# A decode block with a KV cache on one core: eight early stores to the output and two extra loads of x on ScalarE's queue

## The chip, the cores and the metric

The kernel runs on one core of a Trainium2 chip. The metric is the device time of one execution, in microseconds, as the median of several runs. The profile is of one execution of its own, taken by the hardware profiler.

## What is computed

One token per batch row goes through a block: a layer norm of x, attention over a cache of 32768 tokens (32 query heads on 8 heads of keys and values), a gated MLP on the same normed x, and the product of both added to x.

```python
B, Sq, D = 2, 1, 512
Hq, Hkv, Sk, Dh = 32, 8, 32768, 128          # k_cache, v_cache: (B, Hkv, Sk, Dh), float32
...
F = 1792                                     # W_gate, W_up: (D, F); W_down: (F, D)
...
xn = _layernorm(x, axis=-1)
q = (xn @ wq) per head
scores = q k^T * Dh ** -0.5
o = softmax(scores) v
s = o @ wo
gate, up = xn @ W_gate, xn @ W_up
g = silu((gate * (gate > 0) * up) @ W_down)
out = x + s * g
```

The output has 2 x 512 floats, 4 KB.

## The kernel before, in words

The program is written as a list of operations (`pg.op`), each with the engine that carries it out and the names of what it reads and writes. From these names the program works out the semaphore waits: an operation that reads a name waits for the operation that last wrote it, and one that writes a name waits for its last writer and for all who read it since. Each engine then carries out its own operations in the order in which they were listed. A DMA counts on a semaphore of its own (`load(dst, src, sem, ...)` at L239 and L240), 16 for each transfer, and the engine named in `engine=` issues it; all DMA instructions carry the line L240 of the helper, all plain matmuls the line L243.

SyncE (SP) issues all the large loads, in this order: wq (8.4 MB, into `wide`), the first pair of key tiles (8.4 MB, into `k0`), W_gate and W_up (3.7 MB each, into `wide` when the query's products are done with wq), the second pair of key tiles (`k1`), W_down (`load_d`, into `wide` when the gate and up products are done), the third pair of keys, and from there on a pair of value tiles and a pair of key tiles in turn, 32 pairs of each. There are two buffers for keys (`kbuf`) and one for all the rest (`wide`), so a load is issued when its buffer comes free, and waits in the queue behind the loads ahead of it. At the end come the parts of wo and the store of the result.

ScalarE issues the two small loads of x at the start (`xp`, two rows for the layer norm, and `xy`, the same 4 KB in eight rows for the last addition), then takes the square root of the layer norm (L374), later the silu (L648) and the exponentials of the softmax (L722).

The start of the work, as the engines carry it out: VectorE fills constants (`perm`, L291 and L333; `spread` in st3, L341), takes the mean and variance of x (L364 to L372), and behind the square root normalizes x (L378, L380). TensorE turns it (L391) and multiplies by wq in two halves (`project_q`, into m_ps0 and m_ps1). VectorE copies the halves to SBUF (L481: the first into os0, the second into os1), TensorE gathers the heads, VectorE copies them (L498 qd, L517 qall), and GpSimd makes the first group's query qcur (L530). Then VectorE turns the keys in place, 8 transposes for a pair of tiles (L660), TensorE makes the scores, and behind the first two tiles' scores the gate and up products (`mlp_gu`, into m_ps), whose end sets free `wide` for W_down. L580 and the lines behind it make the hidden layer, `mlp_down` and `mlp_fold` the gate g.

os1 is also `ot`, in which each group's heads are turned (L803). perm and st3 are read by TensorE; st3 is written again by the scores of the fourth tile (L678).

Of the kernel before, what the change touches and what calls it, by code (L numbers as in the profile page):

```python
# [8 lines left out]
P = 128  # L9
# [153 lines left out]
def decode_block_kernel(nc, x, kc, vc, wq, wo, wg, wu, wd, out):  # L163
# [17 lines left out]
    def sbuf(name, *shape, align=32):  # L181
        return nc.alloc_sbuf_tensor(name, list(shape), F32, align_bytes=align)[:]
# [6 lines left out]
    st = [sbuf(f"st{i}", P, NR * Q) for i in range(NU)]  # L189
# [7 lines left out]
    perm = sbuf("perm", P, 4, Q // REP, REP)  # L197
# [5 lines left out]
    gy = sbuf("gy", P, P)  # L203
# [18 lines left out]
    ot = os_[1]  # L222
# [7 lines left out]
    def dve(fn, r=(), w=()):  # L230
        pg.op("DVE", fn, r, w)
# [7 lines left out]
    def load(dst, src, sem, r=(), w=(), engine="SP"):  # L239
        pg.op(engine, lambda e: e.dma_start(dst, src), r, w, dma=sem)  # L240
# [22 lines left out]
    def of_columns(t):  # L263
        return t[0:P:APART, :]

    def by_column(t):
        return t.rearrange("b s (c n) -> c (b s) n", c=4)
# [5 lines left out]
            out=ident,  # L273
# [23 lines left out]
    for kb in range(4):  # L297
        dve(
            lambda e, kb=kb: e.memset(block_of[Q * kb : Q * kb + Q, kb * REP : (kb + 1) * REP], 1.0),
            w=["block_of"],  # L300
# [27 lines left out]
    n = 1  # L328
    while n < Q:
# [45 lines left out]
        ["stat", "eps"],  # L375
        ["stat"],
    )
    dve(lambda e: e.reciprocal(stat[:, 4:5], stat[:, 3:4]), ["stat"], ["stat"])  # L378
    dve(
        lambda e: e.tensor_scalar(xc, xc, stat[:, 4:5], None, op0=ALU.mult),  # L380
# [467 lines left out]
    def project_far():  # L848
        parts = []
        for j in range(ROWS - 4, ROWS):  # L850
            parts.append((ots[:, 1, j, :], WO[1][:, j, :], [*its_heads(1), WOK[1, j]]))
        parts.insert(2, (fold, py_sb, ["fold", "os0"]))
        for n, (o, w, held) in enumerate(parts):
            pe(
                chain(
                    [
                        mm(
                            far[32 * c : 32 * c + 32, :P],
                            o,
                            w[:, c * P : (c + 1) * P],  # L860
                            n == 0,
                            n == len(parts) - 1,
                        )
                        for c in range(4)
                    ]
                ),
                held,
                ["s1"],
            )
        dve(lambda e: e.tensor_mul(gy, far[:, :P], gy), ["s1", "gy"], ["gy"])  # L870
        dve(
            lambda e: e.tensor_add(gy, gy, xy),  # L872
            ["gy", "xy"],
            ["gy"],
        )
# [6 lines left out]
    for j in range(PAIRS + 2):  # L882
        s, v = 2 * j, 2 * (j - 2)
# [51 lines left out]

    project_near(range(2, NEAR))
    project_far()
    load(by_column(out), of_columns(gy), "out", r=["gy"])

    sems = {s: nc.alloc_semaphore(f"sem_{s}") for s in pg.count}  # L940
    with nc.Block(no_gpsimd_drain=True) as block:
# [54 lines left out]
```

## Time and profile before

| | us |
|---|---|
| median of 3 runs | 1311.1 (1309.98 to 1311.5) |
| span of the profiled execution, first to last instruction | 1308.4 |
| TensorE busy (matmul) | 859.0 |
| VectorE busy | 718.1 |
| ScalarE busy | 51.4 |
| GpSimd busy | 10.5 |

The profiled execution's own time is known as its span; the median of the runs is 2.7 us longer, which holds what lies ahead of the first and behind the last instruction. The core moves 564.79 MB, at 432 GB/s in the mean over the span. Queue q1 is that of SyncE, q10 that of ScalarE, q8 and q14 carry instructions. In rows of the timeline the first number is the start in us, the second the time it took, and the brackets hold how long the engine had been idle before and what it waited for; SPq and ACTq rows are DMAs being issued. In rows of the DMA queues the numbers are the packets that started in the window asked for, their MB, and the time that they took as a share of the 16 engines' time in that window (over 100% where a packet ends behind the window).

### The profile page before, as it was taken

What the parts mean: (1) busy time and instruction counts of PE and PEld (TensorE: products, weight loads), DVE (VectorE), ACT (ScalarE), POOL (GpSimd) and SP (SyncE); (2) the same over time, 40 slices, a digit from 0 to 9 for tenths busy, and PEclk for the clock granted to TensorE, in tenths of its full rate; (3) what the DMA queues carried; (4) which work ended last, traced back from release to release, by engine and by line L of the source; (5) the groups of instructions that cost most, each with busy time, mean ns of one, the idle gap of its engine ahead of it and who ended that gap; (6) DMA issues with size and microseconds to landing.
All of it is one profiled execution on the core that took longest, in us unless ns stands there. A gap on an engine that the chain in (4) does not pass through costs nothing.

```text
span 1308.4 us, 11146 instructions
## 1 busy us (share of the span) xinstructions
PE 859.0 (66%) x4720; PEld 211.5 (16%) x4720; DVE 718.1 (55%) x690; ACT 51.4 (4%) x133; POOL 10.5 (1%) x38
## 2 busy tenths in 40 slices
PE   3566675785666587576667667667665757865676
PEld 1111111211111121111111112121111112111121
DVE  3566654565655456664546666455665545656521
ACT  0001000000000000000000000000000000000000
POOL 0000000000000000000000000000000000000000
PEclk9677788878878887878898778798887889788788
DMA  9999999999999999999999999999999999999998
GB/s 417 423 438 435 437 431 441 425 439 429 437 429 439 435 433 441 429 441 427 439 429 437 429 439 435 433 441 429 441 427 439 429 437 429 439 435 433 439 431 357
DMA packets 10693, 564.79 MB, mean 432 GB/s; under 512 B 1195, under 2 KB 1211, under 8 KB 1597
## 3 DMA queue, kind: packets, MB, share of 16 engines
q1 hardware_dynamic: 10668, 564.67, 99.7%
q8 instruction: 6, 0.10, 0.0%
q14 instruction: 3, 0.02, 0.0%
q10 hardware_dynamic: 16, 0.01, 0.0%
HBM read 564.67 MB, written 0.00 MB: 432 GB/s over the span
## 4 chain that ended last, share of the span: by engine, by line
DMA 64%; DVE 17%; PE 15%; issue 4%; SPq 0%
DMA k<-in_A_k_cache_dram 58%; DVE k L660 17%; PE o L243 8%; PE s L243 6%; DMA k<-in_A_wo_dram 3%; DMA w<-in_A_wq_dram 2%; PE m_ps L243 1%; PE m_ps L693 0%; PE d L243 0%; SPq L240 0%; DVE gy L870 0%; DVE gy L872 0%
## 5 line engine op out<-in xcount | busy, mean ns | idle before, releaser
L243 PE MATMUL s<-k,qcur 128*32 128x512 f32 x2048 | 504.5, 710 | 370.5 <-DVE k L660 370.3
L660 DVE STREAM_TRANSPOSE k<-k 128x2048 f32<-128x2048 f32 x256 | 565.2, 2275 | 147.0 <-DMA k<-in_A_k_cache_dram 147.0
L243 PE MATMUL o<-w,wt 128*16 128x512 f32 x1984 | 245.5, 596 | 9.0 <-DMA w<-in_A_v_cache_dram 9.0
L243 PEld LDWEIGHTS s<-k,qcur 128*32 128x32 f32 x2048 | 89.5, 123 | 785.0 <-DVE k L660 639.3
L737 DVE STREAM_TRANSPOSE wt<-pt 128x512 f32<-128x512 f32 x64 | 45.9, 717 | 139.4 <-PE pt L243 134.6
L678 DVE TENSOR_SCALAR_CACHE_REDUCE st<-s 128x512 f32<-128x512 f32 x64 | 43.0, 672 | 120.9 <-PE s L243 120.9
L243 PEld LDWEIGHTS o<-w,wt 128*16 128x16 f32 x1984 | 62.4, 98 | 167.5 <-issue 167.5
L722 ACT ACTIVATE st<-st,nb 128x512 f32<-128x512 f32 x64 | 45.4, 710 | 1111.0 <-DVE nb L719 1111.0
L243 PE MATMUL pt<-st,perm 128*128 128x512 f32 x128 | 72.6, 696 | 1.5 <-ACT st L722 1.5
L763 DVE RECIPROCAL rl<-m_ps 128x1 f32<-128x1 f32 x16 | 2.7, 169 | 111.0 <-PE m_ps L243 111.0
L243 PE MATMUL m_ps<-ob,heads 128*128 128x128 f32 x128 | 21.7, 321 | 29.0 <-DVE ob L777 29.0
L243 PEld LDWEIGHTS pt<-st,perm 128*128 128x128 f32 x128 | 25.3, 219 | 34.4 <-issue 30.1
L803 DVE STREAM_TRANSPOSE os<-m_ps 128x512 f32<-128x512 f32 x16 | 11.5, 717 | 23.2 <-PE m_ps L243 23.2
L243 PEld LDWEIGHTS m_ps<-ob,heads 128*128 128x128 f32 x128 | 18.0, 217 | 31.1 <-DVE ob L777 31.1
L243 PE MATMUL m_ps<-w,wt 128*32 128x512 f32 (+1 forms) x128 | 16.2, 640 | 8.1 <-DMA w<-in_A_wq_dram 8.1
L777 DVE SCALAR_TENSOR_TENSOR ob<-o,share,ob 128x128 f32<-128x128 f32 x48 | 16.9, 351 | 1.7
L530 POOL TENSOR_TENSOR qcur<-qall,block_of 128x128 f32<-128x128 f32 x16 | 6.5, 406 | 1008.3 <-PE s L243 974.0
L243 PE MATMUL m_ps<-negone,mrow 1*128 1x1 f32 x32 | 6.0, 256 | 9.3 <-DVE mrow L708 9.3
L722 ACT ACTIVATION_READ_ACCUMULATOR st<-st,nb 128x1 f32 x64 | 11.9, 186 | 0.0
L481 DVE COPY os<-m_ps 128x512 f32<-128x512 f32 x2 | 1.4, 692 | 16.3 <-PE m_ps L243 16.3
L243 PE MATMUL o<-k,wt 128*16 128x512 f32 x64 | 8.4, 687 | 2.8 <-DMA k<-in_A_v_cache_dram 2.8
L391 PE MATMUL m_ps<-ident,st 32*128 32x32 f32 x4 | 0.7, 307 | 14.0 <-DVE st L380 14.0
(80 smaller groups left out, 102.8 us busy)
## 6 DMA issues: line engine op xcount, KB each, us to landing
k<-in_A_wo_dram SPq DMA_DIRECT2D x1, 4096.0 KB, 37.3
w<-in_B_W_gate_dram SPq DMA_DIRECT2D x1, 3584.0 KB, 19.6
w<-in_B_W_up_dram SPq DMA_DIRECT2D x1, 3584.0 KB, 27.6
w<-in_B_W_down_dram SPq DMA_DIRECT2D x1, 3584.0 KB, 15.6
k<-in_A_wo_dram SPq DMA_DIRECT2D x1, 2048.0 KB, 41.7
k<-in_A_wo_dram SPq DMA_DIRECT2D x1, 1024.0 KB, 43.7
k<-in_A_k_cache_dram SPq DMA_DIRECT2D x32, 48.2
k<-in_A_wo_dram SPq DMA_DIRECT2D x1, 512.0 KB, 44.5
```

The lines of the kernel that those rows point to most:

```text
L243: return lambda e: e.matmul(out_, lhs, rhs, start=start, stop=stop, skip_group_check=True)
L391: lambda e, k=k: e.transpose(px[:, k * 32 : (k + 1) * 32], xquad[:, k, :], ident[:32, :32])
L481: dve(lambda e, q=qs, h=half: e.tensor_copy(q, pq[h]), [f"m{half}"], [f"os{half}"])
L530: lambda e: e.tensor_tensor(qcur.rearrange("p e (k h) -> p e k h", h=REP), qall[:, b, hk].unsqueeze(2).to_broadcast([P, 4, Q // REP, REP]) ...
L660: dve(lambda e: e.transpose(at_, at_), [f"k{t // 2 % 2}"], [key])
L678: lambda e: e.tensor_scalar(st[u], ps_s[t % 2], SCALE, None, op0=ALU.mult, op1=ALU.max, accum_out=mx[:, u : u + 1],),
L722: lambda e, u=u: e.activation(st[u], st[u], AF.Exp, bias=nb, scale=1.0, accum_out=ls[:, u : u + 1]),
L737: dve(lambda e: e.transpose(wt[t % 2], ps_p[t % 2]), [f"pt{t % 2}"], [f"wt{t % 2}"])
L763: dve(lambda e: e.reciprocal(rl, ps_m[1][:, :1]), ["m1"], ["rl"])
L777: lambda e, part=part, c=c: e.scalar_tensor_tensor(ob, part, share[:, c : c + 1], ob, op0=ALU.mult, op1=ALU.add),
L803: lambda e: e.transpose(ot, ps_m[1].rearrange("p (h q j) -> p j h q", h=REP, j=ROWS)),
```

## The change

ScalarE issues ten more DMAs behind its square root, in the list of operations between L377 and L378 of before. Eight are stores to the output, in six different shapes of the two sides: from eight rows of perm that lie 16 partitions apart, from the first eight rows of perm, from four rows of it, and from two rows of st3. The two last are loads of x into os1, once into eight rows next to each other and once into rows 16 apart. All ten count on one semaphore, `early`. Each store names "out" as what it writes, each load "os1". The result's store, which overwrites the whole output at the end, now names "out" too. Nothing else is changed.

```diff
+    zeros = perm.rearrange("p a b c -> p (a b c)")
+
+    def in_rows(t):
+        return t.rearrange("b s (c n) -> (b s c) n", c=4)
+
+    def early(dst, src, r, w):
+        load(dst, src, "early", r=r, w=w, engine="ACT")
+
+    one_batch = out[0, 0].rearrange("(c n) -> c n", c=4)
+    early(by_column(out), of_columns(zeros), ["perm"], ["out"])
+    early(by_column(out), of_columns(zeros), ["perm"], ["out"])
+    early(by_column(out), zeros[0:8, :], ["perm"], ["out"])
+    early(in_rows(out), of_columns(zeros), ["perm"], ["out"])
+    early(in_rows(out), zeros[0:8, :], ["perm"], ["out"])
+    early(one_batch, zeros[0:P:32, :], ["perm"], ["out"])
+    early(one_batch, zeros[0:4, :], ["perm"], ["out"])
+    early(out.rearrange("b s d -> (b s) d"), st[3][0:2, :], ["st3"], ["out"])
+    early(ot[0:8, :P], in_rows(x), [], ["os1"])
+    early(of_columns(ot[:, :P]), in_rows(x), [], ["os1"])
     dve(lambda e: e.reciprocal(stat[:, 4:5], stat[:, 3:4]), ["stat"], ["stat"])
...
-    load(by_column(out), of_columns(gy), "out", r=["gy"])
+    load(by_column(out), of_columns(gy), "out", r=["gy"], w=["out"])
```

Here `by_column` is the output's view as 4 x 2 x 128, `of_columns` every 16th partition of a tile. The second writer of os1 in the program's start is VectorE's copy of the query's second half (L481 of before, L500 after the change).

## The prediction

> **What bounds the kernel now.** I read the page first: the share of the DMA, the queues, and the chain of work that ended last.
>
> ```profile
> span 1308.4 us, 11146 instructions
> ...
> DMA  9999999999999999999999999999999999999998
> ...
> q1 hardware_dynamic: 10668, 564.67, 99.7%
> ...
> q10 hardware_dynamic: 16, 0.01, 0.0%
> ...
> DMA 64%; DVE 17%; PE 15%; issue 4%; SPq 0%
> ```
>
> SyncE's queue q1 keeps the 16 DMA engines busy for 99.7% of the span. So the kernel is one stream of 564.67 MB, and time that this stream stands idle can't be made up later. ScalarE's queue q10 carries only the two small loads of x. A change that adds no bytes worth counting can move the time in one way: by making the stream run dry. I therefore ask when the next load must be issued, and on whom it waits. The timeline of the first 45 us shows the start:
>
> ```profile
> 0.74 0.39 SPq L240 DMA_DIRECT2D w<-in_A_wq_dram  x1
> ...
> 1.42 1.19 ACTq L240 DMA_DIRECT2D st<-in_A_x_dram  x1
> ...
> 2.66 0.60 ACTq L240 DMA_DIRECT2D xy<-in_A_x_dram  x1
> ...
> 10.13 0.68 DVE L364 TENSOR_REDUCE stat<-st 32x1 f32<-32x512 f32 x1 [2.91 <-DMA st<-in_A_x_dram]
> ...
> 12.95 0.29 ACT L374 ACTIVATE stat<-stat,eps_t 32x1 f32<-32x1 f32 x1 [8.38 <-DVE stat L372]
> ...
> 32.04 0.69 DVE L481 COPY os<-m_ps 128x512 f32<-128x512 f32 x1 [2.74 <-PE m_ps L243]
> ...
> 33.90 0.22 DVE L498 COPY qd<-pt 128x64 f32<-128x64 f32 x1 [1.16 <-PE pt L243]
> ...
> 35.32 0.42 DVE L517 COPY qall<-pt 128x256 f32<-128x256 f32 x1 [1.20 <-PE pt L243]
> ...
> 43.31 17.66 DVE L660 STREAM_TRANSPOSE k<-k 128x2048 f32<-128x2048 f32 x8 [7.57 <-DMA k<-in_A_k_cache_dram]
> ```
>
> The second L481 (the copy of m_ps1 into os1, at 32.04) is done in time: VectorE is through with the query at 35.74 and then waits 7.57 us for the first keys. The timeline from 60 to 80 us shows the place where the stream first depends on this work:
>
> ```profile
> 66.08 6.28 PE L243 MATMUL m_ps<-w,wt 128*32 128x448 f32 x58
> ...
> 72.39 0.33 SPq L240 DMA_DIRECT2D w<-in_B_W_down_dram  x1
> 72.76 1.28 SPq L240 DMA_DIRECT2D k<-in_A_k_cache_dram  x1
> ...
> 79.54 17.67 DVE L660 STREAM_TRANSPOSE k<-k 128x2048 f32<-128x2048 f32 x8 [4.36 <-DMA k<-in_A_k_cache_dram]
> ```
>
> W_down may only be issued when TensorE has used up the gate and up weights (72.39). The load in flight then, the second pair of keys, lands at 79.5. That is the slack: 7.1 us, less the time from issue to first packet.
>
> **What the change puts where.** On ScalarE ten DMAs come behind the square root (L374 before and after):
>
> ```order
>  L240 DMA xy<-in_A_x_dram 8x1x128 [waits sem_DVE]
>  L374 ACT_TABLE_LOAD
>  L374 ACTIVATE stat<-stat,eps_t 32x1 [waits sem_DVE]
> ...
> +L240 DMA out_dram<-perm 4x2x128
> +L240 DMA out_dram<-perm 4x2x128 [waits sem_early] x2
> +L240 DMA out_dram<-perm 8x128 [waits sem_early] x2
> +L240 DMA out_dram<-perm 4x128 [waits sem_early] x2
> +L240 DMA out_dram<-st 2x512 [waits sem_early]
> +L240 DMA os<-in_A_x_dram 8x128
> +L240 DMA os<-in_A_x_dram 8x128 [waits sem_early]
> ```
>
> Each store but the first waits until the one before has landed, because all of them write "out"; the first load goes right behind the eighth store, the second waits for both. That is nine waits for a landing in a row, counting the last one, which falls to VectorE (L481 of before is L500 of after):
>
> ```order
> -L481 COPY os<-m_ps 128x512 [waits sem_PE] x2
> -L498 COPY qd<-pt 128x64 [waits sem_PE]
> ...
> +L500 COPY os<-m_ps 128x512 [waits sem_PE]
> +L500 COPY os<-m_ps 128x512 [waits sem_early,sem_PE]
> +L517 COPY qd<-pt 128x64 [waits sem_PE]
> ```
>
> The loads write os1, so the copy into os1 waits for all ten. Behind it on VectorE are qd, qall and every transpose of keys; behind those TensorE's scores and the gate and up products; behind these SyncE's issue of W_down. Nothing else waits: ScalarE's own next work, the silu of L648, needs what W_down is multiplied with, and SyncE's last store carries no wait for the early ones, since what VectorE has told it covers them. The ten transfers' bytes (under 40 KB) are nothing beside 564 MB.
>
> Let E be the time at which the tenth transfer has landed. From L481 to the issue of W_down before lie 72.39 - 32.04 = 40.35 us, of which 7.57 were the wait for keys that would be over: 32.8 us of work. After the change W_down is issued at E + 32.8 and its first packets go about 1.0 us later (SyncE's first load was issued at 0.74; the row of 1.7 to 1.8 us, below, holds the first packets). The stream's slowest engine was free at 79.5, the others some 2 us earlier (the row of 76 to 77 us below: three packets start, where 16 engines start one every 2.4 us, so most have begun their last). The stream stands still from there to E + 33.8: a loss of E - 45.7 for the slowest engine and E - 43.8 for the rest, say **E - 45**. Below E = 45 the change is free; this far the wait of 7.57 us and the queue's stock cover it. Once W_down runs, VectorE is 2 us behind the stream's restart, as it was before (77.6 to 79.54), so the rest goes as before, only later.
>
> **What one landing costs.** The trace has two near rows. Without other traffic: the result's store, the same 4x2x128 shape as the first three.
>
> ```profile
> 1306.60 0.69 SPq L240 DMA_DIRECT2D out_dram<-gy  x1
> ```
>
> The span ends at 1308.4, so 1.8 us. Under the stream: x's first load, issued at 1.42 and used at 10.13, so 8.7 us. Nine times the one is 16 us, nine times the other 78. The packets per queue in windows of the trace tell which holds; first 1.7 to 1.8, then q1 and q10 in five windows of 1 us that start at 7.0, 9.4, 11.8, 14.2 and 16.6, then 46 to 48, 76 to 77, and 1306 to 1308.4 us:
>
> ```profile
> q1 hardware_dynamic: 5, 0.33, 979.2%
> ...
> q1 hardware_dynamic: 16, 1.05, 241.9%
> q10 hardware_dynamic: 4, 0.01, 1.4%
> ...
> q1 hardware_dynamic: 16, 1.05, 241.9%
> q10 hardware_dynamic: 4, 0.00, 0.5%
> ...
> q1 hardware_dynamic: 16, 1.05, 241.9%
> q10 hardware_dynamic: 4, 0.00, 0.5%
> ...
> q1 hardware_dynamic: 16, 1.05, 241.8%
> q10 hardware_dynamic: 2, 0.00, 0.3%
> ...
> q1 hardware_dynamic: 16, 1.05, 241.9%
> q10 hardware_dynamic: 2, 0.00, 0.1%
> ...
> q1 hardware_dynamic: 31, 0.89, 102.9%
> ...
> q1 hardware_dynamic: 3, 0.20, 45.4%
> ...
> q1 hardware_dynamic: 12, 0.00, 0.7%
> ```
>
> Each window holds one packet of q1 per engine: 1.05 MB / 16 = 65.5 KB, 2.42 us long. Between two of them an engine serves one packet of q10, however small. The counts 4, 4, 4, 2, 2 fit 2 engines with 1 data packet and 1 closing packet for the first load of x, then 4 engines with 2 and 1 for the second; the result's store has 12 packets, again 4 times (2 + 1). So a transfer under this stream costs one round of 2.42 us per packet, and it has to get in first: x's first load was issued at 1.42, its first packet went in the window at 7.0, so it missed the round one 2.42 us earlier, near 4.8. I read this as one packet of q1 being taken ahead. In a chain the next store is issued about 1.5 us after the last one's closing packet (its closing packet went in the window at 9.4 and the reader began at 10.13, so some tenths until the waiter goes on; 0.6 to issue, as for the second load of x; then the way to the queue, within the 1.0 of SyncE's first load), so it misses the next turn and gets the one after. A two-packet transfer then costs 3 rounds, a three-packet one 4.
>
> Rounds are 2.42 us while wq and keys stream, 1.06 us for the gate and up weights (102.9% x 16 x 2 us / 31). Per engine an 8.4 MB load (128 rows of 64 KB) has 8 packets of 65.5 KB, a gate or up load (3.67 MB in 128 rows) 8 of 28.7 KB (0.89 MB / 31). Counted from the first packets at 1.7 to 1.8, with 8 rounds a load: wq to 21.9, keys to 41.3, gate and up to 58.3, the second keys to 77.7. Now the chain, from the square root's end at 13.24:
>
> Store 1 (three packets) stands behind the second load of x on engines 0 and 1, whose last packet goes near 17: data 19.4 and 21.9, closing with the end of wq, landed between 22 and 24.4. Stores 2 and 3, the same shape: 4 rounds each, about 9.7 us, so about 32 to 34 and 41.4. Stores 4 to 7 have two packets (one row per engine; this count is an estimate from the shapes) and meet the short rounds: 4 x 1.06 = 4.2 us each (the 1.5 us on the way use up two rounds), so 45.6, 49.9, 54.1, 58.3. Store 8 on long rounds: 3 x 2.42 = 7.3, 65.6. The first load follows on the same queue, two rounds more: 70.4. The second load: 7.3 more, **E = 78**. The loss is 78 - 45 = **33 us**: span 1308.4 + 33 = 1341.4, and with the 2.7 us by which the median of the runs (1311.1) lies above this span, **1344 us**. The bounds of a landing are the rows of 1.8 and 8.7 us.
>
> **The rivals.**
>
> *No packet taken ahead.* If a store gets the first turn after it is issued, every long transfer saves one round: 22 to 24, 31, 38, 42, then 3.2 us each in the short rounds (45, 48, 51, 55), the first load 57 and the second 61. E = 61, loss 16: 1327 us. For it: the first load of x may only have been slow on its way (its issue took 1.19 us, the second's 0.60). Against: the second load, too, missed the round near 5, and SyncE's own first packet came within 1.0 us of its issue.
>
> *Each landing costs what it costs on free engines: not slower.* Nine times 1.8 from 13.3 gives 29.5, before L481 at 32.04: 1311 us, no change. This decides as soon as a landing costs under (45 - 13.3) / 9 = 3.5 us in the mean. For it: the q10 packets themselves last hundredths of a us. Against: the windows above, where each waits 2.42 us for its turn, and the 8.7 us of the first load. The Trainium skill has a rule that gives this outcome: "DMA: Bandwidth & Descriptors", Anatomy of one DMA, puts a DMA at about 2.0 us fixed plus its bytes at 436 GB/s; by that estimate the chain ends near 31 and costs nothing. This trace's 8.7 us beside a full stream disagrees with it.
>
> *More than one packet ahead.* Then every landing costs a round more, and the chain meets the end of the stream at 77.7 with transfers left, which then land in 1.8 us each: with two or three left E = 82 to 84, 1348 to 1350 us. For it: nothing beyond the loose fit of one observation. The same skill page, Queues, rings and completion order, says that an engine goes round its queues by whole packets and gives 9 to 17 descriptors as typical for one; were the eight 65.5 KB records of a load one such packet, a turn would take 19 us and this rival would hold. The windows show a q10 packet after each single 65.5 KB record, so I give it little.
>
> That the change doesn't chain its transfers I exclude: the rows above carry the waits, and the value VectorE waits for in the code is that of all ten.
>
> **The numbers.** Forecast (E = 76 to 80) 0.55; no packet ahead, or only some turns missed (E = 58 to 75) 0.26; more ahead 0.11; as on free engines, no change 0.07; faster 0.01, for which I see no mechanism. A measurement of this kernel can tell about 0.2%, 2.6 us, from no change. Slower 0.92, same 0.07, faster 0.01. The range takes the forecast with its bounds, most of the no-packet-ahead case and the lower end of more ahead: 1325 to 1350 us.
>
> **What would show it.** In the timeline of the changed kernel: the second copy into os1 starts near 78 and names a DMA as what it waited for; W_down is issued near 111; a hole in the DMA share of the slices near 80 to 112 us; the stores' issues on ScalarE 4 us apart between 41 and 58 and 7 to 10 us apart elsewhere; after 112 the same pace as before. Issues 2 us apart, or a second copy at 32, would prove me wrong, and so would a hole without the full loss in the time: then the stream has slack that I don't see.

## The result and the profile after

| | before | after |
|---|---|---|
| median, us | 1310.5 (1309.8 to 1311.5, 4 runs) | 1348.1 (1347.8 to 1348.8, 4 runs) |
| ratio, 95% interval | | 1.029 (1.028 to 1.030) |
| span of the profiled execution | 1308.4 | 1346.2 |

The kernel is 37.6 us slower; the forecast was 33 us more (1344), with a range of 1325 to 1350. The span grew by 37.8 us. The page of the changed kernel, same lines as shown of before:

```profile
span 1346.2 us, 11157 instructions
...
DMA  9926999999999999999999999999999999999998
...
q1 hardware_dynamic: 10668, 564.67, 96.9%
...
q10 hardware_dynamic: 136, 0.05, 0.0%
...
DMA 62%; DVE 19%; PE 14%; issue 4%; SPq 0%; ACTq 0%; DVEq 0%; ACT 0%
```

The stream's 10668 packets are the same; its share fell because there is now a hole in the third and fourth of the 40 slices (each 33.7 us). Busy time by stretches says how deep it is. The rows hold the stretch, the busy time of each engine, the granted clock, the DMA share and GB/s; first after, then before:

```profile
0.00:78.00 78.00, 10.66 (x76) 3.98 (x76) 9.62 (x38) 1.58 (x2) 0.70 (x6) 0.74 0.97 417
78.00:114.00 36.00, 24.43 (x144) 9.51 (x144) 21.40 (x18) 1.28 (x1) 0.41 (x1) 0.76 0.01 1
150.00:1346.00 1196.00, 802.99 (x4391) 195.29 (x4391) 658.72 (x611) 43.93 (x120) 8.96 (x30) 0.83 1.00 432
```

```profile
0.00:78.00 78.00, 36.43 (x220) 12.20 (x220) 33.27 (x58) 2.86 (x3) 1.10 (x7) 0.85 0.99 422
78.00:114.00 36.00, 22.77 (x109) 5.31 (x109) 26.01 (x22) 4.58 (x10) 0.41 (x1) 0.78 1.01 439
```

For the 36 us from 78 to 114 the DMA moves 1 GB/s instead of 439. Ahead of the hole the stream runs as before (417 GB/s against 422), behind 150 us at the old mean of 432. The loss lies in this one hole. From the timeline after: what ScalarE does until then, one row for each of its DMA issues behind the square root, then VectorE's copy into os1 and SyncE's issue of W_down:

```profile
13.14 0.61 ACTq L240 DMA_DIRECT2D out_dram<-perm  x1
22.66 0.57 ACTq L240 DMA_DIRECT2D out_dram<-perm  x1
32.18 0.64 ACTq L240 DMA_DIRECT2D out_dram<-perm  x1
41.90 0.62 ACTq L240 DMA_DIRECT2D out_dram<-perm  x1
48.34 0.33 ACTq L240 DMA_DIRECT2D out_dram<-perm  x1
54.51 0.56 ACTq L240 DMA_DIRECT2D out_dram<-perm  x1
63.61 0.26 ACTq L240 DMA_DIRECT2D out_dram<-perm  x1
71.04 0.24 ACTq L240 DMA_DIRECT2D out_dram<-st  x1
71.31 0.30 ACTq L240 DMA_DIRECT2D os<-in_A_x_dram  x1
78.70 0.63 ACTq L240 DMA_DIRECT2D os<-in_A_x_dram  x1
...
80.76 0.69 DVE L500 COPY os<-m_ps 128x512 f32<-128x512 f32 x1 [51.64 <-DMA os<-in_A_x_dram]
...
113.42 0.33 SPq L240 DMA_DIRECT2D w<-in_B_W_down_dram  x1
```

Each issue but the first and the ninth (71.31, right behind the eighth store) comes when the transfer before has landed. The copy into os1 waits 51.64 us, for the loads of x, and starts at 80.76; W_down is issued 113.42 - 80.76 = 32.66 us later.

### The profile page after: what moved, and what is told of

Read it like the earlier page. It is cut to its first block, busy times and chain, and to the rows that moved or that the text cites. A ratio compares the mean times of both kernels' runs of the same rounds, so it can differ in the third digit from the quotient of the medians.

```text
span 1346.2 us, 11157 instructions
## 1 busy us (share of the span) xinstructions
PE 860.0 (64%) x4720; PEld 213.8 (16%) x4720; DVE 717.8 (53%) x690; ACT 51.4 (4%) x133; POOL 10.5 (1%) x38
## 3 DMA queue, kind: packets, MB, share of 16 engines
q1 hardware_dynamic: 10668, 564.67, 96.9%
## 4 chain that ended last, share of the span: by engine, by line
DMA 62%; DVE 19%; PE 14%; issue 4%; SPq 0%; ACTq 0%; DVEq 0%; ACT 0%
DMA k<-in_A_k_cache_dram 53%; DVE k L679 19%; PE o L243 8%; PE s L243 5%; DMA out_dram<-perm 4%; DMA k<-in_A_wo_dram 3%; DMA os<-in_A_x_dram 1%; DMA st<-in_A_x_dram 1%; PE m_ps L243 1%; PE pt L243 0%; PE m_ps L712 0%; SPq L240 0%; DVE wt L612 0%; DVE os L500 0%; DVE st L371 0%
## 5 line engine op out<-in xcount | busy, mean ns | idle before, releaser
L500 DVE COPY os<-m_ps 128x512 f32<-128x512 f32 x2 | 1.4, 691 | 64.9 <-DMA os<-in_A_x_dram 51.6
L243 PE MATMUL pt<-both,os 128*128 128x8 f32 x16 | 2.9, 311 | 48.7 <-DVE os L500 48.7
L243 PEld LDWEIGHTS pt<-both,os 128*128 128x128 f32 x16 | 2.8, 259 | 49.6 <-DVE os L500 48.8
```

The costliest lines, as they stand in the source:

```text
L243: return lambda e: e.matmul(out_, lhs, rhs, start=start, stop=stop, skip_group_check=True)
L500: dve(lambda e, q=qs, h=half: e.tensor_copy(q, pq[h]), [f"m{half}"], [f"os{half}"])
```

## The experiments

The theory: the chain of nine landings in a row, each of which must wait for its turn behind the stream's packets, holds the copy into os1 until E, and the time lost is E less a constant; read from the change, 80.8 - 37.8 = 43. The rivals: the small transfers slow the stream itself; a fixed cost for each transfer; the direction (stores to the output); and, for the size of a landing, other reasons than the packets of the stream. Times are medians, beside runs of before on the same chip (1309.95 and 1310.04 us); ratios are to these.

**The chain without a waiter.** The two loads go to a tile of their own.

```diff
-    early(ot[0:8, :P], in_rows(x), [], ["os1"])
-    early(of_columns(ot[:, :P]), in_rows(x), [], ["os1"])
+    load(aside[0:8, :], in_rows(x), "aside", w=["aside"], engine="ACT")
+    load(of_columns(aside), in_rows(x), "aside", w=["aside"], engine="ACT")
...
-    load(by_column(out), of_columns(gy), "out", r=["gy"], w=["out"])
+    load(by_column(out), of_columns(gy), "out", r=["gy", "aside"], w=["out"])
```

> All ten transfers stay on ScalarE's queue, but the two loads go to a tile of their own that nobody reads, so VectorE's second copy waits for TensorE alone; the result's store waits for the loads. Theory (the chain costs only because the copy into os1 waits for its end): the copy starts at 32 us, W_down is issued near 72, time 1311 us, no change from before. Rival (the small packets, or stores to the output beside the stream, slow the stream itself): the time stays near 1348, or in part.

Measured: 1310.4 us, ratio 1.0003 (0.9993 to 1.0012). From its timeline, ScalarE's last issue, and VectorE's copy:

```profile
79.61 0.63 ACTq L241 DMA_DIRECT2D aside<-in_A_x_dram  x1
...
31.92 0.69 DVE L501 COPY os<-m_ps 128x512 f32<-128x512 f32 x1 [2.74 <-PE m_ps L244]
```

The chain is as long as in the change, to 79.6, and costs nothing. The transfers themselves don't slow the stream; what costs time is that the copy into os1 waits for them.

**The chain made of loads.** Instead of the eight stores, eight loads of x in the same shapes, each waiting for the one before.

```diff
-    early(by_column(out), of_columns(zeros), ["perm"], ["out"])
-    early(by_column(out), of_columns(zeros), ["perm"], ["out"])
+    early(aside[0:P:16, :], by_column(x), [], ["asides"])
+    early(aside[1:P:16, :], by_column(x), [], ["asides"])
...
```

> The loads of x from the run without a chain, in the same shapes, but all eight on one name, so that each waits for the one before, as the stores do. Theory (the chain costs, not the direction): copy near 80, 1345 to 1350 us. Rival (writing to the output's memory makes a landing long): a chain of loads is faster, copy under 70, below 1338 us.

Measured: 1348.0 us, ratio 1.029 (1.027 to 1.031), and the copy starts where it does in the change:

```profile
80.76 0.69 DVE L501 COPY os<-m_ps 128x512 f32<-128x512 f32 x1 [51.27 <-DMA os<-in_A_x_dram]
```

Writing to the output's memory is no part of the cost.

**The same loads without a chain.** Each of the eight has a name of its own (`aside0` to `aside7`); all else is as in the last.

```diff
-    early(aside[0:P:16, :], by_column(x), [], ["asides"])
-    early(aside[1:P:16, :], by_column(x), [], ["asides"])
+    early(aside[0:P:16, :], by_column(x), [], ["aside0"])
+    early(aside[1:P:16, :], by_column(x), [], ["aside1"])
...
```

> The eight stores are replaced by eight loads of x with the same shapes, each into rows of its own, so that none waits for another; the two loads into os1 stay, the second waiting for all nine, and the copy into os1 for all ten. Theory (an engine serves one small packet after each packet of the stream): engines 0 and 1 have 21 packets of the first nine transfers to serve, 12 until 41 us and the rest at 1.06 us each, so the nine have landed near 50, the tenth near 56; loss about 56 - 43 = 13 us, 1324 us. Rival (a landing is a fixed time of 7 to 9 us that overlaps when nothing waits): nine have landed near 28, the tenth near 35, so the copy starts near 35 and the time is 1311. Rival (all is due to the number of transfers): 1348.

Measured: 1325.2 us, ratio 1.012 (1.010 to 1.014).

```profile
50.90 0.59 ACTq L241 DMA_DIRECT2D os<-in_A_x_dram  x1
...
57.30 0.69 DVE L501 COPY os<-m_ps 128x512 f32<-128x512 f32 x1 [27.68 <-DMA os<-in_A_x_dram]
```

The nine that don't wait for each other have landed at 50.9, as counted from one small packet per round (50), not at 28. So even without waits small transfers through one queue take turns with the stream; the chain adds the way from issue to first packet for each. It makes up 80.8 - 57.3 = 23.5 us of E.

**A shorter chain.** Stores 4 to 8 are left out.

```diff
-    early(in_rows(out), of_columns(zeros), ["perm"], ["out"])
-    early(in_rows(out), zeros[0:8, :], ["perm"], ["out"])
-    early(one_batch, zeros[0:P:32, :], ["perm"], ["out"])
-    early(one_batch, zeros[0:4, :], ["perm"], ["out"])
-    early(out.rearrange("b s d -> (b s) d"), st[3][0:2, :], ["st3"], ["out"])
```

> Only the first three stores and the two loads are left. Theory: the third store lands at 41.9 as measured, the first load just behind it near 43, the second 6.3 us later; the copy into os1 starts near 50, and by the measured loss of the change (copy at 80.8, 37.6 us) the loss is 50 - 43 = 7 us, 1317 to 1319 us. Rival (the loss goes with the number of transfers, 5 of 10): 19 us, 1329. Rival (the stream's first stop costs a fixed sum): over 1330.

Measured: 1316.5 us, ratio 1.005 (1.004 to 1.007).

```profile
49.38 0.69 DVE L494 COPY os<-m_ps 128x512 f32<-128x512 f32 x1 [20.12 <-DMA os<-in_A_x_dram]
```

Half the transfers cost 6.5 us of 37.6: the cost isn't by transfer. It begins where the slack ends.

**A longer chain.** Four more stores behind the eighth.

```diff
+    for _ in range(4):
+        early(out.rearrange("b s d -> (b s) d"), st[3][0:2, :], ["st3"], ["out"])
```

> Four more stores of the eighth's shape stand in the chain between the eighth store and the loads. Theory (turns cost time only while the stream runs; it is dry from 78 us on in the change): the eighth store still lands near 78, and each transfer behind it takes the 2.1 us that the tenth took there; the copy into os1 starts near 89 instead of 80.8, loss 89 - 43 = 46 us, 1356 us. Rival (a store costs its 7.4 us wherever it stands): copy near 111, 1378 us.

Measured: 1353.1 us, ratio 1.033 (1.031 to 1.035).

```profile
71.41 0.24 ACTq L240 DMA_DIRECT2D out_dram<-st  x1
...
78.59 0.24 ACTq L240 DMA_DIRECT2D out_dram<-st  x1
79.81 0.24 ACTq L240 DMA_DIRECT2D out_dram<-st  x1
81.03 0.24 ACTq L240 DMA_DIRECT2D out_dram<-st  x1
...
85.82 0.69 DVE L502 COPY os<-m_ps 128x512 f32<-128x512 f32 x1 [55.89 <-DMA os<-in_A_x_dram]
```

The first row is the eighth store, which still takes 7.2 us (71.41 to 78.59). Once the stream is dry the same store takes 1.22 us. My 2.1 for it came from the tenth transfer (8 rows), so the copy's start was missed by 3 us, and the direction stands: load on the engines makes the landing long, not the transfer.

**All ten transfers in another order.** The two loads come first, on a semaphore of their own.

```diff
+    load(ot[0:8, :P], in_rows(x), "first", w=["os1"], engine="ACT")
+    load(of_columns(ot[:, :P]), in_rows(x), "first", w=["os1"], engine="ACT")
     early(by_column(out), of_columns(zeros), ["perm"], ["out"])
...
-    early(ot[0:8, :P], in_rows(x), [], ["os1"])
-    early(of_columns(ot[:, :P]), in_rows(x), [], ["os1"])
```

> All ten transfers of the change in another order: the two loads into os1 first, on a semaphore of their own, then the chain of eight stores. Theory (only the landing that the copy into os1 waits for counts): the second load lands near 30, before the copy at 32; the last store lands near 90, before VectorE writes st3 again at 101; 1311 us, no change from before. Rival (ten transfers behind the square root cost their time somewhere in any order): over 1320 us.

Measured: 1309.9 us, ratio 1.000 (0.999 to 1.001). The last store is issued at 82.3, and the copy no longer waits for it:

```profile
82.30 0.24 ACTq L240 DMA_DIRECT2D out_dram<-st  x1
...
31.85 0.69 DVE L500 COPY os<-m_ps 128x512 f32<-128x512 f32 x1 [2.74 <-PE m_ps L243]
```

**Shorter packets in the stream, twice.** First wq and the first two pairs of keys in four DMAs each, so that packets have 16 KB; then each in two DMAs whose runs of 4 KB take turns.

```diff
+    def load_in_four(dst, src, sem, keys):
+        n = dst.shape[1] // 4
+        for i in range(4):
+            cut = slice(i * n, (i + 1) * n)
+            load(dst[:, cut], src[:, cut], f"{sem}_{i}", w=[*(keys if i == 3 else []), f"{sem}_{i}"])
...
-        load(kbuf[b], rows_of(kc, 2 * j), f"k{b}", w=k_keys(b))
+        if j < 2:
+            load_in_four(kbuf[b], rows_of(kc, 2 * j), f"kk{b}", k_keys(b))
+        else:
+            load(kbuf[b], rows_of(kc, 2 * j), f"k{b}", w=k_keys(b))
```

> The change as it is, but wq and the first two pairs of keys are each loaded in four pieces of a quarter of the columns, so that the packets of the stream are 16 KB instead of 64. The bytes and the order of the loads are the same. Theory (a landing pays for turns behind the stream's packets): rounds of 0.6 us, a landing some 3.5 to 4 us, the ten have landed at 45 to 55, loss 2 to 12 us, 1313 to 1323 us. Rival (a landing's 7 to 9 us is the time of the store's own path under load, whatever the packets): the copy stays near 80, 1348 us.

Measured: 1331.9 us, ratio 1.017 (1.015 to 1.019). VectorE's copy:

```profile
64.10 0.69 DVE L512 COPY os<-m_ps 128x512 f32<-128x512 f32 x1 [34.93 <-DMA os<-in_A_x_dram]
```

This lies between the two expectations: shorter packets help, and not nearly by as much as one packet taken ahead would have it. A part of the gain is not the chain's: the first load of x lands earlier too, so the first store goes out at 10.12 us instead of 13.14. From there to the copy it is 54.0 us instead of 67.6. The second kernel's edit, `load_by_turns`, stands in the same places:

```diff
+    def load_by_turns(dst, src, sem, keys):
+        for i in range(2):
+            d, s = (t.rearrange("p (a t n) -> p t a n", t=2, n=1024)[:, i] for t in (dst, src))
+            load(d, s, f"{sem}_{i}", w=[*(keys if i == 1 else []), f"{sem}_{i}"])
```

> As with the pieces of 16 KB, but the rows of wq and of the first two pairs of keys go in runs of 4 KB, so that a packet of the stream lasts some 0.15 us. With 64, 28 and 16 KB packets the first packet of a store came 3.5 to 4.8 us after its issue. If a few packets are taken ahead (about four of 16 KB), it now comes within 2 us, a landing takes 2.5 us, and the copy into os1 starts near 38: 1311 us. If a fixed amount of data or a fixed time under load lies ahead, it still comes after 3.5 to 4 us, a landing takes some 4.5 to 5 us, and the copy starts at 58 to 64: 1325 to 1331 us.

Measured: 1328.9 us, ratio 1.014 (1.012 to 1.016), as the second of the two expectations had it. Its second and third store, and the copy:

```profile
16.28 0.56 ACTq L240 DMA_DIRECT2D out_dram<-perm  x1
22.35 0.64 ACTq L240 DMA_DIRECT2D out_dram<-perm  x1
...
63.70 0.69 DVE L511 COPY os<-m_ps 128x512 f32<-128x512 f32 x1 [29.20 <-DMA os<-in_A_x_dram]
```

The copy's start decides here, and not the time: with packets of 4 KB the stream itself is slower. In the first 30 us it moves 329 GB/s (before: 420), and it stops only near 88 us:

```profile
0.00:30.00 30.00, 3.02 (x16) 1.23 (x20) 8.93 (x37) 1.58 (x2) 0.70 (x6) 1.00 0.93 329
78.00:88.00 10.00, 6.95 (x45) 1.53 (x49) 9.22 (x6) 0.00 (x0) 0.00 (x0) 1.00 0.86 321
88.00:97.00 9.00, 8.32 (x82) 3.62 (x74) 1.97 (x5) 0.00 (x0) 0.00 (x0) 1.00 0.02 4
```

By an estimate from the stop at 88 instead of 78 this kernel would have been some 10 us slower than before with a short chain too, so the first expectation's 1311 us was out of reach either way; its copy at 38 was not.

Queues of the same kernel in two windows, 16.0 to 20.4 us and 20.5 to 21.0 us:

```profile
q1 hardware_dynamic: 365, 1.50, 101.5%
...
q1 hardware_dynamic: 43, 0.18, 92.4%
q10 hardware_dynamic: 3, 0.00, 1.0%
```

The store issued at 16.28 has no packet served until 20.5, while some 365 / 16 = 23 packets of the stream pass on each engine. In the change itself, with 64 KB, the store issued at 22.66 has its first packets in the half microsecond from 26.5 (first row pair below), and the tenth transfer, issued at 78.70 on free engines, in the window 80.1 to 80.4 (last row):

```profile
q1 hardware_dynamic: 13, 0.85, 392.9%
q10 hardware_dynamic: 4, 0.00, 1.4%
...
q10 hardware_dynamic: 16, 0.00, 5.7%
```

So it is about 4 us from issue to first packet under load, whether that means one or two packets of 64 KB or 23 of 4 KB, and 1.4 us on free engines. The number of packets isn't what counts. The 2.6 us between may be a fixed amount of data that an engine has taken on ahead (2.6 us at 65.5 KB in 2.42 us is about 70 KB) or a time on the way; the runs don't tell these apart.

## Why the prediction was right, and where its sizes were off

**The mechanism held.** The loss is one hole in the stream, opened by the copy into os1 that waits for all ten transfers; the run without a waiter and the run with the loads first take it away whole. W_down's issue at E + 32.8 was measured at E + 32.66. E was forecast at 78 and came at 80.8.

**The loss for a given E was 2 us too small.** The step "a loss of E - 45.7 for the slowest engine and E - 43.8 for the rest, say E - 45" took a value between the two. Over the profiled runs:

| | E, us | growth of the span, us | difference |
|---|---|---|---|
| three stores | 49.4 | 6.2 | 43.2 |
| loads without a chain | 57.3 | 14.0 | 43.3 |
| 4 KB packets | 63.7 | 20.4 | 43.3 |
| 16 KB packets | 64.1 | 21.2 | 42.9 |
| the change | 80.8 | 37.8 | 43.0 |
| four more stores | 85.8 | 43.3 | 42.5 |

E - 43 holds for all, also in the row of 4 KB packets, where the stream itself is slower: W_down is issued 32.65 us behind the copy there too (96.35), and the rest follows from that. For the changed kernel the 2 us can be counted from the trace. Queue q1 from 75.0 to 75.8, from 114.0 to 115.3 and from 116 to 117 us:

```profile
q1 hardware_dynamic: 16, 1.05, 302.2%
...
q1 hardware_dynamic: 16, 0.46, 130.9%
...
q1 hardware_dynamic: 16, 0.46, 106.2%
```

The last 16 packets of keys, one per engine, start between 75.0 and 75.8 and last 302.2% x 0.8 = 2.42 us each, so none ends later than 78.2. The engine that was free only at 79.5, from which the forecast took its E - 45.7, is not there. Ten of these 16 packets start by 75.3, and ten of the next 16 by 114.6. That is 39.3 us; less the 2.42 us of the last packet it is a standstill of 36.9 us, or E - 43.9, close to the forecast's E - 43.8 for the rest of the engines. The other part is a slow start, which the forecast put at nothing: the first packets take 130.9% x 1.3 = 1.70 us each, the same packets later 1.06. These 0.6 us and the standstill make 37.5 of the 37.8 us. A row that the prediction shows had such a start already: the stream's very first packets take 979.2% x 16 x 0.1 / 5 = 3.1 us instead of 2.42. Its "wq to 21.9" comes out only with it, since eight rounds of 2.42 us from 1.75 end at 21.1. No run took the slow start away, so its part is counted and not tested.

**Stores 1 to 3 were right, 4 to 7 forecast too short, the rest too long.** Landings of the first three stores were forecast near 22 to 24.4, 32 to 34 and 41.4; the issues behind them came at 22.7, 32.2 and 41.9. "4 x 1.06 = 4.2 us each" for the short rounds failed: measured 6.4 and 6.2, then 9.1 for the sixth, which ran into the long packets again, and 7.4 for the seventh, which stood among them. The reason is the step "I read this as one packet of q1 being taken ahead": under 64 KB packets one packet and 2.4 us are the same, under shorter ones it is the time that stays. In the other direction, the eighth store and the first load behind it, counted at 12.1 us (58.3 to 70.4), had both landed 7.4 us after the load's issue, and the tenth transfer, counted at 7.3 us, took 2.1: both met the end of the stream at 78. In all, stores 4 to 7 were forecast 12.2 us too short and the last three transfers 10.0 us too long. So it is in good part luck that E was forecast within 2.8 us. With the loss term's 2 us the forecast of the span (1341.4) lies 4.8 us low. The median's (1344) lies only 4.1 low, because the runs come out 1.9 us above the profiled span here, and not 2.7.

**The rivals.** Without a packet ahead (E = 61) fell with the issues 9.5 us apart. As on free engines (no change) fell by the same rows; the 1.2 to 2.1 us of a landing after 78 show that its price is right only where nothing else runs. The 2 us that this rival names from the Trainium skill, "DMA: Bandwidth & Descriptors", Anatomy of one DMA, are given there for DMAs that GpSimd issues; here ScalarE issues them. "More than one packet ahead" gave 1348 to 1350 and so the measured time, and not for its reason: with 64 KB packets no landing cost a round more than forecast, and stores 2 and 3 have the forecast's 9.5 to 9.7 us. Its turn of 19 us behind eight records isn't there either.

## What to carry to other kernels

In this kernel a small DMA beside a stream that fills the engines costs the time from issue to first packet (about 4 us) plus one packet of the stream for each further packet of its own: 6 to 10 us in all, where free engines need 1.2 to 2.1. What a chain of such DMAs costs here depends only on who waits for its end and on how long the stream has loads in stock at that moment: give the buffer that the main path writes next to the first link, not the last, or to none. Transfers that don't have to be ordered should not share a name that the program takes as a write.

## What the runs showed of the hardware

The first packet of a small transfer is served about 4 us after its issue with packets of 64 KB and of 4 KB in the stream alike, against 1.4 us with nothing beside it. Two queues share an engine packet by packet: beside packets of 65.5 KB each further small packet waits 2.42 us, beside packets of 28.7 KB 1.06 us (by this count the nine loads without a chain were expected at 50, and had landed at 50.9). A stream that has stood still for 36 us begins again with packets of 1.70 us instead of 1.06. With packets of 4 KB the stream moved 329 GB/s in its first 30 us, with 64 KB 420.
